# Opening of an attention block: silu moved to VectorE, one tile normalized by ScalarE, the third query copied by VectorE, the warm-up matmuls and first loads rearranged, and TensorE's usual path placed behind its branch without a jump

## The chip, the cores and the metric

One core of one Trainium2 chip. The metric is the device time of one execution in microseconds (us); lower is better. An execution also has a span, the stretch that the profile covers; the time is about 1.7 to 1.9 us more than the span.

## The reference, cut to what matters

```python
mod = (_silu(c) @ w_mod).reshape(c.shape[0], 6, 1, -1)      # c: 1 x 512, w_mod: 512 x 3072
sa, ca, ga, sb, cb, gb = ...                                # six rows of 512
h = _layernorm(x) * (1 + ca) + sa                           # x: 2048 x 512
x = x + ga * _A_ref(h, k_cache, v_cache, wq, wo)            # 32 query heads, 8 key heads of 128,
                                                            # softmax over the last 512 keys
h = _layernorm(x) * (1 + cb) + sb
x = x + gb * _B_ref(h, w1, w2)                              # relu MLP of width 1792
```

The first score matmul needs three things: x normalized, transposed, scaled and shifted; the scale and shift (`sa`, `ca`), which need silu(c) and a megabyte of `w_mod`; and the first query weights. That opening is what the change is about. At the other end, the softmax is computed without subtracting a maximum; a flag says whether that was safe, and each engine branches on it before its last instructions (TensorE at 510.6 us of the 559.4 in the profile below).

## The kernel before

TensorE is PE, VectorE DVE, ScalarE ACT, GpSimd POOL, SyncE SP; SP and ACT issue the loads. The program keeps one list of instructions for each engine; `reads` and `writes` become semaphores.

```python
def load_wm01(i, eng=None):                  # half of the shift and scale weights, 512 KB
    c0, c1 = i * DC // 2, (i + 1) * DC // 2
    dma(wm01[:, c0:c1, :], wm01v[:, c0:c1, :], f"wm{i}", writes=[R_wm[i]], eng=eng)

def warm(n):                                 # the warm-up: matmuls on ones
    for i in range(n):
        mm(bank[WBK], ones[:, :], ones[:, 0:1].to_broadcast([P, QB]), True, True, [R_ones], [WBK], i == n - 1)

def silu_mul():                              # c / (1 + exp(-c)); the power -1 by cst[:, 3:4]
    kb.op(POOL, ... tensor_scalar(tmp, tmp, 1e38, 1.0, op0=min, op1=add))
    kb.op(POOL, ... tensor_tensor(tmp, tmp, cst[:, 3:4], op=pow))
    kb.op(POOL, ... tensor_tensor(sc_bf, c_f, tmp, op=mult))
# ... cut ...
    load_wm01(0); load_wm01(1, ACT); load_wq(0, 2, ACT); load_wq(2, 2); load_k(0); load_v(0)
    warm(7)
    silu_exp(5)                              # transpose of c on PE; exp and copy on ACT
    warm(9)
    # ... ACT: sum and sum of squares of tile 3 ...
    silu_mul()
    ln_stat(0); ln_stat(1)                   # DVE
    rstd_add(0, 2); rstd_pow(0, 2)           # DVE, then POOL: (var + eps) ** -0.5
    ln_stat(2)
    rstd_add(2, 3); rstd_pow(2, 4)
    ln_norm(0); ln_norm(1)                   # DVE; tile 3 is normalized by POOL
    ln_tposes(0, TB[0])                      # transposes on PE
    for f in mod_cols_mm(0, QBK): f()        # 32 one-column matmuls: shift and scale
    ln_norm(2)
    mod_cols_evac(0, QBK)
    # ... transposes of tiles 1 to 3, scaling (hT), first two queries (qT) ...
# ... cut ...
def engine(name, e):
    kb.emit(stream, e, 0, n_ops)
    # ... wait for the flag ...
    v = e.value_load(flag[0:1, 0:1])
    with e.If(v != 128):                     # never in these runs
        kb.emit(stream, e, n_ops)
        # ... all engines meet ...
        gkb.emit(general[name], e)           # the general kernel, long
    with e.Else():
        kb.emit(stream, e, n_ops)            # the last part
```

Of the kernel before, what the change touches and what calls it, by code (L numbers as in the profile page):

```python
# [8 lines left out]
ACTF = mybir.ActivationFunctionType  # L9
# [1189 lines left out]
def build_fast(nc, es, top, A_x, A_k_cache, A_v_cache, A_wq, A_wo, B_x, B_w1, B_w2, c, w_mod, out, flag):  # L1199
    P = 128  # L1200
# [98 lines left out]
    def dma(out_ap, in_ap, key, reads=(), writes=(), transpose=False, eng=None):  # L1299
        k = dsem(key)  # L1300
        if transpose:
            return kb.op(SP, lambda e: e.dma_start_transpose(out_ap, in_ap), reads=reads, writes=writes, dma_sem=k)
        return kb.op(eng or SP, lambda e: e.dma_start(out_ap, in_ap), reads=reads, writes=writes, dma_sem=k)  # L1303
# [14 lines left out]
    R_h0 = RL("h0", DC)  # L1318
    R_q1 = RL("q1_", 2)
    R_cf, R_m01 = Res("cf"), Res("m01")  # L1320
    R_s3, R_eps = Res("s3"), Res("eps")
# [28 lines left out]
    def load_wm01(i, eng=None):  # L1350
        c0, c1 = i * DC // 2, (i + 1) * DC // 2
        dma(wm01[:, c0:c1, :], wm01v[:, c0:c1, :], f"wm{i}", writes=[R_wm[i]], eng=eng)

    def wm_res(sl, cc):
        return R_wm[cc // (DC // 2)] if sl < 2 else R_wm[sl]

# [5 lines left out]
    def load_mlp(i):  # L1362
        if not wm_done:
            wm_done.extend(all_events(R_wm))
        f0 = i % (FC // 2) * 2
        if i < FC // 2:
            kb.op(SP, lambda e: e.dma_start(w1_sb[:, :, f0 * P:(f0 + 2) * P], w1v[:, :, f0 * P:(f0 + 2) * P]), writes=R_w1[f0:f0 + 2], pre=wm_done, dma_sem=dsem(f"w1{f0}"))
        else:
            kb.op(SP, lambda e: e.dma_start(w2_sb[:, f0:f0 + 2, :], w2v[:, f0:f0 + 2, :]), writes=R_w2[f0:f0 + 2], pre=wm_done, dma_sem=dsem(f"w2{f0}"))
# [6 lines left out]

    def warm(n):
        for i in range(n):
            mm(bank[WBK], ones[:, :], ones[:, 0:1].to_broadcast([P, QB]), True, True, [R_ones], [WBK], i == n - 1)

# [39 lines left out]
    def silu_mul():  # L1420
        kb.op(POOL, lambda e: e.tensor_scalar(tmp[:, :], tmp[:, :], 1e38, 1.0, op0=ALU.min, op1=ALU.add), reads=[R_tmp], writes=[R_tmp])
        kb.op(POOL, lambda e: e.tensor_tensor(tmp[:, :], tmp[:, :], cst[:, 3:4].to_broadcast([P, DC]), op=ALU.pow), reads=[R_tmp, R_eps], writes=[R_tmp])
        kb.op(POOL, lambda e: e.tensor_tensor(sc_bf[:, :], c_f[:, :], tmp[:, :], op=ALU.mult), reads=[R_tmp, R_cf], writes=[R_sc])

# [52 lines left out]
    def q_mms(u, bk=QBK):  # L1477
        b, h = units[u]
        for i, cc in enumerate(range(DC)):
            mm(bank[bk], wq_sb[:, cc, h * Dh:(h + 1) * Dh], hT[b % 2][:, cc, :], i == 0, i == DC - 1,  # L1480
               [R_wq[h], R_hT[b % 2][cc]] + ([R_h0[cc]] if b == 0 else []), [bk], i == DC - 1)
        q_evac(u, bk)

    def q_evac(u, bk=QBK):
        kb.op(ACT, lambda e: e.activation(qT[u % NQT][:, :], bank[bk], ACTF.Copy), reads=[R_b[bk]], writes=[R_qT[u % NQT]])  # L1485

# [74 lines left out]
    dma(c_row[:, :], c[0].rearrange("(c p) -> c p", p=P), "c", writes=[R_c])  # L1561
    load_wm01(0)
    load_wm01(1, ACT)
    load_wq(0, 2, ACT)
    load_wq(2, 2)
    load_k(0)
    load_v(0)
    kb.op(POOL, lambda e: e.memset(ones[:, :], 1.0), writes=[R_ones])
    kb.op(POOL, lambda e: e.memset(cst[:, 0:1], -0.5), writes=[R_cst])
# [7 lines left out]
    kb.op(ACT, lambda e: e.activation(cst[:, 2:3], cst[:, 0:1], ACTF.Exp), reads=[R_cst], writes=[Res("dummy")])  # L1577
    warm(7)
    silu_exp(5)
    warm(9)  # L1580
    t3 = TPB - 1
    kb.op(ACT, lambda e: e.activation(xn[:, t3, :], x_sb[:, t3, :], ACTF.Copy, accum_out=s3[:, 0:1]), reads=[R_x[t3]], writes=[R_xn[t3], R_s3])
    kb.op(ACT, lambda e: e.activation(s3[:, 1:2], s3[:, 0:1], ACTF.Copy, scale=-1.0 / D), reads=[R_s3], writes=[R_s3])
    kb.op(ACT, lambda e: e.activation(xn[:, t3, :], x_sb[:, t3, :], ACTF.Square, bias=s3[:, 1:2], accum_out=s3[:, 2:3]), reads=[R_x[t3], R_s3], writes=[R_xn[t3], R_s3])
    kb.op(ACT, lambda e: e.activation(rstd[:, t3:t3 + 1], s3[:, 2:3], ACTF.Identity, scale=1.0 / D, bias=cst[:, 1:2]), reads=[R_s3, R_eps], writes=[R_rstd[t3]])
# [7 lines left out]

    silu_mul()
    ln_stat(0)
    ln_stat(1)
    rstd_add(0, 2)
    rstd_pow(0, 2)
    ln_stat(2)
    rstd_add(2, 3)  # L1600
    rstd_pow(2, 4)
    ln_norm(0)
    ln_norm(1)
    kb.op(POOL, lambda e: e.tensor_scalar(xn[:, t3, :], x_sb[:, t3, :], s3[:, 1:2], rstd[:, t3:t3 + 1], op0=ALU.add, op1=ALU.mult),
# [9 lines left out]

    ln_tposes(0, TB[0])
    fs = mod_cols_mm(0, QBK)
    for f in fs:
        f()
    ln_norm(2)
    mod_cols_evac(0, QBK)  # L1620
# [13 lines left out]
    def q_half(u, hf, order, bk):  # L1634
        for cc in order:
            mm(bank[bk][:, hf * HB:(hf + 1) * HB], wq_sb[:, cc, u * Dh:(u + 1) * Dh], hT[0][:, cc, hf * HB:(hf + 1) * HB], cc == CC_ORDER[0], cc == CC_ORDER[-1],
               [R_wq[u], R_half[hf][cc]], [bk], cc == CC_ORDER[-1])

    for tl in range(1, TPB):
        ln_tposes(tl, TB[tl // 2])  # L1640
    mod_half(0, 0, DVE)
    mod_half(0, 2, ACT)
    mod_half(0, 1, DVE)
    mod_half(0, 3, ACT)
# [61 lines left out]
    def h1_group(b, fc):  # L1706
        dst, r = h2_of[b]
        bk = hb_banks[cnt["h"] % len(hb_banks)]
        cnt["h"] += 1
        for cc in range(DC):  # L1710
            mm(bank[bk], w1_sb[:, cc, fc * P:(fc + 1) * P], dst[:, cc, :], cc == 0, cc == DC - 1, [R_w1[fc], r[cc]], [bk], cc == DC - 1)
        kb.op(ACT, lambda e: e.activation(h1T[b % 2][:, fc, :], bank[bk], ACTF.Relu), reads=[R_b[bk]], writes=[R_h1[b % 2][fc]],  # L1712
              pre=all_events(R_wq) if b < 2 else ())

# [86 lines left out]
def bass_adaLN_cond__sliding_block_cached__dense_activation_relu__prompt_kernel(  # L1801
# [14 lines left out]
    with ExitStack() as top:  # L1816
# [5 lines left out]
        with ExitStack() as es:  # L1822
            gkb, general = build_general(nc, es, *args)

            def engine(name, e):
                stream, n_ops = fast[name], cut[name]
                kb.emit(stream, e, 0, n_ops)
                e.wait_ge(sems[flag_ev[0]], flag_ev[1])
                v = e.value_load(flag[0:1, 0:1])
                with e.If(v != 128):  # L1830
                    kb.emit(stream, e, n_ops)
                    if stream.cnt:
                        e.wait_ge(sems[name], stream.cnt)
                    if name == "sp":
                        for k, n in dma_cnt.items():
                            e.wait_ge(sems[k], n)
                    e.sem_inc(meet, 1)
                    e.wait_ge(meet, len(fast))
                    gkb.emit(general[name], e)
                with e.Else():  # L1840
                    kb.emit(stream, e, n_ops)

# [50 lines left out]
```

## Time and profile before

| | before |
|---|---|
| time, median of 3 (lowest to highest) | 560.52 us (560.33 to 560.81) |
| the profiled execution: time, span | 561.1, 559.4 us |
| first value product's weights loaded at | 16.47 us |
| last VectorE instruction to the end of the span | 2.02 us |

The first value product is the first matmul of softmax times V. From there to the branch TensorE is dense, so this moment measures the opening. The lines of the page and of the chain are in the prediction.

### The profile page before, as it was taken

What the parts mean: (1) busy time and instruction counts of PE and PEld (TensorE: products, weight loads), DVE (VectorE), ACT (ScalarE), POOL (GpSimd) and SP (SyncE); (2) the same over time, 40 slices, a digit from 0 to 9 for tenths busy, and PEclk for the clock granted to TensorE, in tenths of its full rate; (3) what the DMA queues carried; (4) which work ended last, traced back from release to release, by engine and by line L of the source; (5) the groups of instructions that cost most, each with busy time, mean ns of one, the idle gap of its engine ahead of it and who ended that gap; (6) DMA issues with size and microseconds to landing.
All of it is one profiled execution on the core that took longest, in us unless ns stands there. A gap on an engine that the chain in (4) does not pass through costs nothing.

```text
span 559.4 us, 9666 instructions
## 1 busy us (share of the span) xinstructions
PE 550.5 (98%) x4060; PEld 315.8 (56%) x4134; DVE 253.8 (45%) x551; ACT 348.9 (62%) x453; POOL 54.7 (10%) x53
## 2 busy tenths in 40 slices
PE   8999999999999999999999999999999999999998
PEld 4665555555555555555555555555555654444444
DVE  4455555553546544335445443333354448321134
ACT  4986666666666666666666666666666644432500
POOL 3000022004410000033000000332000000000000
DMA  9897763513114144352352412111215110210001
GB/s 268 248 207 174 143 169 46 114 39 76 40 38 76 39 73 117 58 133 57 94 95 57 76 40 39 39 39 38 39 39 76 39 30 0 44 34 23 22 29 47
DMA packets 113309, 42.67 MB, mean 76 GB/s; under 512 B 93928, under 2 KB 112104, under 8 KB 113256
## 3 DMA queue, kind: packets, MB, share of 16 engines
q1 hardware_dynamic: 112024, 40.82, 34.3%
q10 hardware_dynamic: 1232, 1.15, 0.6%
q8 instruction: 33, 0.54, 0.4%
q14 instruction: 20, 0.16, 0.1%
HBM read 18.35 MB, written 2.10 MB: 37 GB/s over the span
## 4 chain that ended last, share of the span: by engine, by line
PE 98%; issue 1%; DMA 1%; DVE 0%; SPq 0%; DVEq 0%
PE psS L1372 28%; PE psO L1372 27%; PE psQ L1372 23%; PE psW L1372 20%; DMA c_row<-in_c_dram 1%; DVE qT L1611 0%; DVE hT L1630 0%; SPq L1303 0%; DVE PT L1723 0%; DVE PT L1725 0%; PE psS L1375 0%; PE psO L1416 0%; DVE modc L1438 0%; DVEq L123 0%
## 5 line engine op out<-in xcount | busy, mean ns | idle before, releaser
L1493 ACT ACTIVATE PT<-psS 128x1024 bf16<-128x1024 f32 x256 | 262.7, 1028 | 128.2 <-PE psS L1372 128.1
L1372 PE MATMUL psS<-qT,kT 128*128 128x512 bf16 x508 | 150.9, 379 | 0.5 <-DVE qT L1611 0.4
L1372 PEld LDWEIGHTS psO<-v,PT 128*128 128x128 bf16 x2048 | 126.6, 98 | 30.2
L1372 PE MATMUL psO<-v,PT 128*128 128x129 bf16 x2048 | 137.0, 220 | 0.0
L1372 PE MATMUL psQ<-hT,wq 128*128 128x512 bf16 (+1 forms) x510 | 130.5, 377 | 0.3 <-DVE hT L1630 0.2
L1503 DVE RECIPROCAL rinv<-psO 128x4 f32<-128x4 f32 x128 | 23.3, 182 | 227.2 <-PE psO L1372 227.2
L1372 PE MATMUL psW<-wo,oT 128*128 128x512 bf16 x454 | 118.1, 379 | 3.0
L1504 DVE TENSOR_TENSOR o<-psO,rinv 128x512 bf16<-128x512 f32 x128 | 88.5, 691 | 4.9 <-DVE rinv L1503 0.5
L1372 PEld LDWEIGHTS psQ<-hT,wq 128*128 128x128 bf16 x512 | 49.9, 98 | 60.3 <-issue 0.6
L1372 PEld LDWEIGHTS psS<-qT,kT 128*128 128x128 bf16 x512 | 49.5, 98 | 58.9 <-ACT PT L1493 0.7
L1485 ACT ACTIVATE qT<-psQ 128x512 bf16<-128x512 f32 x126 | 74.7, 593 | 0.0
L1712 ACT ACTIVATE wq<-psS 128x512 bf16<-128x512 f32 x56 | 33.4, 597 | 49.3 <-PE psS L1372 48.9
L1372 PEld LDWEIGHTS psW<-wo,oT 128*128 128x128 bf16 x512 | 45.0, 98 | 32.9 <-DVE acc L1526 1.2
L1526 DVE TENSOR_TENSOR acc<-psW,acc 128x512 f32<-128x512 f32 x48 | 33.2, 691 | 6.5 <-PE psW L1372 6.5
L1372 PE MATMUL psO<-wmw,wq 128*128 128x512 bf16 (+1 forms) x165 | 32.8, 352 | 0.3
L1529 POOL TENSOR_TENSOR acc<-acc,gaf 128x512 f32<-128x512 f32 x12 | 15.6, 1303 | 146.7 <-DVE acc L1526 139.8
L1388 POOL TENSOR_TENSOR rstd<-rstd,cst 128x4 f32<-128x4 f32 x7 | 7.2, 1025 | 216.8 <-DVE rstd L1387 216.8
L1723 DVE TENSOR_TENSOR PT<-psO,gbf 128x512 f32<-128x512 f32 (+1 forms) x12 | 7.5, 624 | 40.4 <-PE psO L1372 40.4
L1372 PE MATMUL psS<-h2T,wmw 128*128 128x512 bf16 x109 | 25.0, 379 | 0.2
L1372 PEld LDWEIGHTS psO<-wmw,wq 128*128 128x128 bf16 x168 | 15.3, 98 | 16.5
L1372 PE MATMUL psS<-hT,wmw 128*128 128x512 bf16 x110 | 24.4, 379 | 0.1
L1382 DVE BATCH_NORM_STATS2 st<-x 128x6 f32<-128x512 bf16 x31 | 21.1, 681 | 4.8 <-DMA x<-in_A_x_dram 4.8
(85 smaller groups left out, 192.6 us busy)
## 6 DMA issues: line engine op xcount, KB each, us to landing
wo<-in_A_wo_dram SPq DMA_DIRECT2D x4, 1024.0 KB, 5.9
wq<-in_A_wq_dram SPq DMA_DIRECT2D x7, 512.0 KB, 4.6
wmw<-in_B_w_dram SPq DMA_DIRECT2D x14, 256.0 KB, 3.1
wmw<-in_w_mod_dram SPq DMA_DIRECT2D x5, 512.0 KB, 4.8
oT<-o SPq DMA_TRANSPOSE x128, 2.4
out_dram<-PT SPq DMA_DIRECT2D x15, 128.0 KB, 1.7
x<-in_A_x_dram SPq DMA_DIRECT2D x3, 512.0 KB, 4.3
v<-in_A_v_cache_dram SPq DMA_DIRECT2D x8, 128.0 KB, 3.8
```

Source lines behind the costliest of these rows:

```text
L1372: kb.op(PE, lambda e: e.matmul(out_ap, lhsT, rhs, start=start, stop=stop), reads=reads, group_writes=[R_b[k] for k in bk], signal=signal)
L1382: kb.op(DVE, lambda e: e.bn_stats(st[:, t, :], x_sb[:, t, :]), reads=[R_x[t]], writes=[R_st[t]])
L1388: kb.op(POOL, lambda e: e.tensor_tensor(rstd[:, sl], rstd[:, sl], cst[:, 0:1].to_broadcast([P, hi - lo]), op=ALU.pow), reads=R_rstd[sl] + ...
L1485: kb.op(ACT, lambda e: e.activation(qT[u % NQT][:, :], bank[bk], ACTF.Copy), reads=[R_b[bk]], writes=[R_qT[u % NQT]])
L1493: kb.op(ACT, lambda e: e.activation(PT[u % NPT][:, pr * 2:pr * 2 + 2, :], s_ps[pr][:, :, :], ACTF.Exp, scale=scale), reads=[R_b[pr * 2], R ...
L1503: kb.op(DVE, lambda e: e.reciprocal(rinv[:, u, :], o_ps[:, :, P]), reads=[R_b[5], R_b[6]], writes=[R_rinv])
L1504: kb.op(DVE, lambda e: e.tensor_tensor(o_sb[u % NOS][:, :, :], o_ps[:, :, 0:P], rinv[:, u, :].unsqueeze(2).to_broadcast([P, TPB, P]), op=A ...
L1526: kb.op(DVE, lambda e: e.tensor_tensor(acc[:, tl, :], bank[WBK], acc[:, tl, :], op=ALU.add), reads=[R_b[WBK], R_acc[tl]], writes=[R_acc[tl]])
L1529: kb.op(eng, lambda e: e.tensor_tensor(acc[:, tl, :], acc[:, tl, :], gaf[:, :], op=ALU.mult), reads=[R_acc[tl], R_ga], writes=[R_acc[tl]])
L1712: kb.op(ACT, lambda e: e.activation(h1T[b % 2][:, fc, :], bank[bk], ACTF.Relu), reads=[R_b[bk]], writes=[R_h1[b % 2][fc]], pre=all_events( ...
L1723: kb.op(DVE, lambda e: e.tensor_tensor(yt[i][:, c0:c1], bank[bk][:, c0:c1], gbf[:, c0:c1], op=ALU.mult), reads=[R_b[bk], R_gb], writes=[R_ ...
```

## The change

Its intent is to take the silu off GpSimd (whose power for it took 1.04 us), to stop warm-up matmuls from holding TensorE (until 8.98) when silu(c) is ready (at 7.12), to spread normalization over three engines, and to spare TensorE a jump (its branch took 3.44 us). The diff, cut to its core:

```diff
     def load_wm01(i, eng=None):
-        c0, c1 = i * DC // 2, (i + 1) * DC // 2
-        dma(wm01[:, c0:c1, :], wm01v[:, c0:c1, :], f"wm{i}", writes=[R_wm[i]], eng=eng)
+        dma(wm01[:, i, :], wm01v[:, i, :], f"wmc{i}", writes=[R_wmc[i]], eng=eng)
...
-    def warm(n):
+    def warm(n, gate=(), bk=7):            # gate: also wait for these
...
     def silu_mul():                        # POOL add, pow, mult -> DVE add, reciprocal, mult
...
     def q_evac(u, bk=QBK):
+        if u == QA:                        # the third query
+            kb.op(DVE, lambda e: e.tensor_copy(qT[u % NQT][:, :], bank[bk]), ...)
+            return
...
-    load_wm01(0)
-    load_wm01(1, ACT)
-    load_wq(0, 2, ACT)
+    for i in range(DC):
+        load_wm01(i, (ACT, SP)[i % 2])
+    for i, eng in enumerate((SP, SP)):     # first query weights in two pieces
+        dma(wq_sb[:, 2 * i:2 * i + 2, 0:QA * Dh], ..., eng=eng)
+    load_k(0)
     load_wq(2, 2)
-    load_k(0)
...
-    kb.op(POOL, ... memset(ones, 1.0))
+    kb.op(DVE, ... memset(ones, 1.0))
...
-    warm(7)
-    silu_exp(5)
-    warm(9)
     # ACT: sum of tile 3
+    warm(10)
+    silu_exp(5)
...
-    silu_mul()
     ln_stat(0)
+    warm(3, [R_mv[0]])
     ln_stat(1)
+    warm(2, [R_mv[1]])
     rstd_add(0, 2)
     rstd_pow(0, 2)
+    kb.op(POOL, ... s3[:, 3:4] = -mean(1) * rstd(1))
+    kb.op(ACT, lambda e: e.activation(xn[:, 1, :], x_sb[:, 1, :], ACTF.Identity, bias=s3[:, 3:4], scale=rstd[:, 1:2]), ...)
+    silu_mul()
     ln_stat(2)
...
-    ln_norm(1)
...
-    ln_tposes(0, TB[0])
     # the 32 matmuls of the modulation
-    ln_norm(2)
+    ln_tposes(0, TB[0])
...
+    ln_tposes(1, TB[0])
+    warm(2, bk=6)
+    ln_norm(2)
...
+                if name == "pe":
+                    with e.If(v == 128):
+                        last_part()
+                    with e.Else():
+                        rerun()
+                else:                      # as before
```

More of the change, by code (lines that the diff above doesn't have):

```diff
@@ L1319, in build_fast @@
     R_q1 = RL("q1_", 2)
+    R_wmc = RL("wmc", DC)
+    R_wqa = RL("wqa", 2)
+    R_nmr = Res("nmr")
     R_cf, R_m01 = Res("cf"), Res("m01")
@@ L1350, in load_wm01 @@
     def load_wm01(i, eng=None):
-        c0, c1 = i * DC // 2, (i + 1) * DC // 2
-        dma(wm01[:, c0:c1, :], wm01v[:, c0:c1, :], f"wm{i}", writes=[R_wm[i]], eng=eng)
+        dma(wm01[:, i, :], wm01v[:, i, :], f"wmc{i}", writes=[R_wmc[i]], eng=eng)
     def wm_res(sl, cc):
-        return R_wm[cc // (DC // 2)] if sl < 2 else R_wm[sl]
+        return R_wmc[cc] if sl < 2 else R_wm[sl]
     def load_wo(j):
@@ L1363, in load_mlp @@
         if not wm_done:
-            wm_done.extend(all_events(R_wm))
+            wm_done.extend(all_events(R_wm + R_wmc))
         f0 = i % (FC // 2) * 2
@@ L1375, in tpose @@
         kb.op(PE, lambda e: e.transpose(out_ap, in_ap, ident[:, :]), reads=list(reads) + [R_ident], group_writes=[R_b[k] for k in bk], signal=signal)
-    def warm(n):
+    def warm(n, gate=(), bk=7):
         for i in range(n):
-            mm(bank[WBK], ones[:, :], ones[:, 0:1].to_broadcast([P, QB]), True, True, [R_ones], [WBK], i == n - 1)
+            mm(bank[bk], ones[:, :], ones[:, 0:1].to_broadcast([P, QB]), True, True, [R_ones] + list(gate), [bk], i == n - 1)
     def ln_stat(t):
@@ L1420, in silu_mul @@
     def silu_mul():
-        kb.op(POOL, lambda e: e.tensor_scalar(tmp[:, :], tmp[:, :], 1e38, 1.0, op0=ALU.min, op1=ALU.add), reads=[R_tmp], writes=[R_tmp])
-        kb.op(POOL, lambda e: e.tensor_tensor(tmp[:, :], tmp[:, :], cst[:, 3:4].to_broadcast([P, DC]), op=ALU.pow), reads=[R_tmp, R_eps], writes=[R_tmp])
-        kb.op(POOL, lambda e: e.tensor_tensor(sc_bf[:, :], c_f[:, :], tmp[:, :], op=ALU.mult), reads=[R_tmp, R_cf], writes=[R_sc])
+        kb.op(DVE, lambda e: e.tensor_scalar(tmp[:, :], tmp[:, :], 1e38, 1.0, op0=ALU.min, op1=ALU.add), reads=[R_tmp], writes=[R_tmp])
+        kb.op(DVE, lambda e: e.reciprocal(tmp[:, :], tmp[:, :]), reads=[R_tmp], writes=[R_tmp])
+        kb.op(DVE, lambda e: e.tensor_tensor(sc_bf[:, :], c_f[:, :], tmp[:, :], op=ALU.mult), reads=[R_tmp, R_cf], writes=[R_sc])
     def mod_cols_mm(which, bk):
@@ L1480, in q_mms @@
             mm(bank[bk], wq_sb[:, cc, h * Dh:(h + 1) * Dh], hT[b % 2][:, cc, :], i == 0, i == DC - 1,
-               [R_wq[h], R_hT[b % 2][cc]] + ([R_h0[cc]] if b == 0 else []), [bk], i == DC - 1)
+               (R_wqa if h < QA else [R_wq[h]]) + [R_hT[b % 2][cc]] + ([R_h0[cc]] if b == 0 else []), [bk], i == DC - 1)
         q_evac(u, bk)
     def q_evac(u, bk=QBK):
+        if u == QA:
+            kb.op(DVE, lambda e: e.tensor_copy(qT[u % NQT][:, :], bank[bk]), reads=[R_b[bk]], writes=[R_qT[u % NQT]])
+            return
         kb.op(ACT, lambda e: e.activation(qT[u % NQT][:, :], bank[bk], ACTF.Copy), reads=[R_b[bk]], writes=[R_qT[u % NQT]])
@@ L1561, in build_fast @@
     dma(c_row[:, :], c[0].rearrange("(c p) -> c p", p=P), "c", writes=[R_c])
-    load_wm01(0)
-    load_wm01(1, ACT)
-    load_wq(0, 2, ACT)
+    for i in range(DC):
+        load_wm01(i, (ACT, SP)[i % 2])
+    for i, eng in enumerate((SP, SP)):
+        dma(wq_sb[:, 2 * i:2 * i + 2, 0:QA * Dh], wqv[:, 2 * i:2 * i + 2, 0:QA * Dh], f"wqa{i}", writes=[R_wqa[i]], eng=eng)
+    load_k(0)
     load_wq(2, 2)
-    load_k(0)
     load_v(0)
-    kb.op(POOL, lambda e: e.memset(ones[:, :], 1.0), writes=[R_ones])
+    kb.op(DVE, lambda e: e.memset(ones[:, :], 1.0), writes=[R_ones])
     kb.op(POOL, lambda e: e.memset(cst[:, 0:1], -0.5), writes=[R_cst])
@@ L1592, in rstd_pow @@
               reads=R_rstd[lo:hi] + [R_cst], writes=R_rstd[lo:hi])
-    silu_mul()
     ln_stat(0)
+    warm(3, [R_mv[0]])
     ln_stat(1)
+    warm(2, [R_mv[1]])
     rstd_add(0, 2)
     rstd_pow(0, 2)
+    kb.op(POOL, lambda e: e.tensor_scalar(s3[:, 3:4], mv[:, 1, 0:1], rstd[:, 1:2], -1.0, op0=ALU.mult, op1=ALU.mult), reads=[R_mv[1], R_rstd[1]], writes=[R_nmr])
+    kb.op(ACT, lambda e: e.activation(xn[:, 1, :], x_sb[:, 1, :], ACTF.Identity, bias=s3[:, 3:4], scale=rstd[:, 1:2]),
+          reads=[R_x[1], R_nmr, R_rstd[1]], writes=[R_xn[1]])
+    silu_mul()
     ln_stat(2)
@@ L1636, in q_half @@
             mm(bank[bk][:, hf * HB:(hf + 1) * HB], wq_sb[:, cc, u * Dh:(u + 1) * Dh], hT[0][:, cc, hf * HB:(hf + 1) * HB], cc == CC_ORDER[0], cc == CC_ORDER[-1],
-               [R_wq[u], R_half[hf][cc]], [bk], cc == CC_ORDER[-1])
-    for tl in range(1, TPB):
-        ln_tposes(tl, TB[tl // 2])
+               [R_wqa[cc // 2], R_half[hf][cc]], [bk], cc == CC_ORDER[-1])
+    ln_tposes(1, TB[0])
+    warm(2, bk=6)
+    ln_norm(2)
     mod_half(0, 0, DVE)
     mod_half(0, 2, ACT)
+    ln_tposes(2, TB[1])
+    ln_tposes(3, TB[1])
     mod_half(0, 1, DVE)
@@ L1712, in h1_group @@
         kb.op(ACT, lambda e: e.activation(h1T[b % 2][:, fc, :], bank[bk], ACTF.Relu), reads=[R_b[bk]], writes=[R_h1[b % 2][fc]],
-              pre=all_events(R_wq) if b < 2 else ())
+              pre=all_events(R_wq + R_wqa) if b < 2 else ())
     def y_group(b, tl, c0=0, c1=D, deng=None):
@@ L1829, in engine, with last_part, rerun @@
                 v = e.value_load(flag[0:1, 0:1])
-                with e.If(v != 128):
+                def last_part():
+                    kb.emit(stream, e, n_ops)
+                def rerun():
                     kb.emit(stream, e, n_ops)
@@ L1839, in engine @@
                     gkb.emit(general[name], e)
-                with e.Else():
-                    kb.emit(stream, e, n_ops)
+                if name == "pe":
[4 more added lines that the diff above has]
+                else:
+                    with e.If(v != 128):
+                        rerun()
+                    with e.Else():
+                        last_part()
             with nc.allow_non_contiguous_dma(reason="tiny c vector load in column layout, value rows of 256 bytes"):
```

## The prediction

> **What bounds the kernel now.** I first read the page's table of busy time. It puts TensorE (PE) at 98%, and its 40 slices show a 9 everywhere but at the two ends.
>
> ```profile
> PE 550.5 (98%) x4060; PEld 315.8 (56%) x4134; DVE 253.8 (45%) x551; ACT 348.9 (62%) x453; POOL 54.7 (10%) x53
> PE   8999999999999999999999999999999999999998
> ```
>
> So only the part before TensorE becomes dense, or a gap in its stream, can change the time. Busy is not useful, though: warm-up matmuls on a tile of ones count as busy. The chain of waits, in order of time, names what sets the opening:
>
> ```profile
> 1.24 3.66 DMA c_row<-in_c_dram
> 4.90 0.05 issue
> 4.95 0.18 PE psO L1416
> 5.13 3.86 PE psW L1372 x9
> 8.98 0.22 PE psS L1375 x4
> 9.21 0.79 PE psQ L1372 x32
> 10.00 0.02 issue
> 10.02 0.18 DVE modc L1438
> ...
> 10.30 0.42 DVE hT L1630
> ...
> 12.55 0.44 DVE qT L1611
> 12.99 0.35 issue
> 13.34 0.38 PE psS L1372
> ```
>
> The columns are start, duration and what. The row of c lands at 4.90; nine warm-up matmuls then hold TensorE until 8.98, although silu(c), needed by the 32 matmuls of the modulation, is ready at 7.12 (POOL's last silu multiply runs 6.92 to 7.12 in the timeline). Modulation, scaling of the transposed tiles (hT), the first projection (psQ) and its copies (qT) follow one another until the first score matmul at 13.34. From there the chain is matmul after matmul: value products of successive units start at 16.84, 19.48, 22.11, 24.75, a step of 2.635 us, which is what 8 matmuls of 0.216 and 16 of 0.057 cost. The stretch 13.34 to 16.84 is 3.50 us for 16 such matmuls, 3.45 us of work: only 0.05 us lost. The tail is equally dense. Hence the time moves by as much as the first score matmul moves, plus a few hundredths.
>
> The timeline of that opening gives the other lanes:
>
> ```profile
> 4.79 0.69 DVE L1382 BATCH_NORM_STATS2 st<-x 128x6 f32<-128x512 bf16 x1 [4.79 <-DMA x<-in_A_x_dram]
> 5.80 1.04 POOL L1422 TENSOR_TENSOR tmp<-tmp,cst 128x4 f32<-128x4 f32 x1
> 7.08 1.51 POOL L1591 TENSOR_TENSOR rstd<-rstd,cst 128x2 f32<-128x2 f32 x2
> 8.70 0.90 POOL L1604 TENSOR_SCALAR xn<-x,s,rstd 128x512 bf16<-128x512 bf16 x1
> ```
>
> GpSimd (POOL) does the silu power in 1.04 us, then two powers for the layer norm (0.75 each), then normalizes tile 3 until 9.60. That lane is free of waits from 5.43 on, so GpSimd is nearly as late as the warm-up.
>
> [...] warm-up weight loads follow at 0.43 us (5.46, 5.89, 6.32 ... 8.02), while later 128x512 matmuls take 0.216 us. The four transposes at 8.98 take 0.22 us, so the full clock came between 8.45 and 8.98. [...] the power takes 1.04 us on GpSimd, against 182 ns for VectorE's 128x4 reciprocal. [...] the trace has 721 ns for the square with a bias. [...] ACT, POOL, SP and DVE take 50 to 72 ns but PE 3440 ns, from 510.6. That ends at 514.05, just before the queued matmuls run out at 514.12; the chain shows 0.03 us of issue there.
>
> **The change, part by part.**
>
> *Warm-up.* It was 7 + 9 matmuls with c's transpose between, and becomes 10, transpose, then 3 and 2 that wait for the statistics of tiles 0 and 1, plus 2 more between transposes. VectorE now fills the ones, so the start stays near 1.0. Cold, ten take 4.27 us, to 5.3; c's transpose is then at 5.3, but ScalarE's exponential is now behind the tile-3 sum and its scaling (about 5.0 to 5.95) anyway. The last five end at 7.0 if the clock is up by then, at 7.9 if not. They no longer hold the modulation until 8.98.
>
> *Silu.* Removed from GpSimd: 0.28 + 1.04 + 0.20 us. Added to VectorE: add, reciprocal, multiply, each 0.17 to 0.18 us and stepping by 0.22. VectorE's statistics of tiles 0 and 1 and the eps add end at 6.70 as before; silu ends near 7.21, within 0.1 us of the old 7.12. So silu itself gains nothing, but tile 2's statistics slip from 6.60 to 7.11, and the add behind them ends at 8.20 instead of 7.69.
>
> *Modulation.* The shift and scale weights arrive in four 256 KB pieces. In the trace the half issued by SP at 1.66 landed 6.3 us later, at 7.96; now ScalarE's queue no longer carries the first query weights beside it, so I take 7.2 to 7.9 for the last piece. The 32 matmuls (0.79 us) end by 8.2, against 10.00.
>
> *GpSimd lane.* First power at 6.75, done 7.50; the small product for ScalarE's bias (0.28, as silu's first step) done near 7.89; second power waits for VectorE's 8.20: 8.25 to 9.00; tile 3 from 9.10 (the old gap was 0.11) to 10.00. It ended at 9.60 before: **0.40 us later**.
>
> *Normalized tiles.* Tile 0 on VectorE 8.12 to 8.53; [...] tile 2 on VectorE behind the second power, 9.04 to 9.45. Transposes of tiles 0, 1, two warm-ups, tile 2 fill TensorE to about 9.7; tile 3's then run 10.05 to 10.27. Before, the last transpose ended at 10.68 in the profile's modelled ends; with the same 0.17 us of drain, now 10.44. VectorE's two first-half scalings run from 9.47, with modulation long ready (8.75), so they no longer sit in front of the second-half ones.
>
> *From there.* Second-half scalings on VectorE, steps of 0.32 and a last of 0.40: 10.47, 10.79, 11.11 to 11.51. Before, the last ended at 11.99: **-0.48 us**. From that end to the first score matmul the old chain needs 13.34 - 11.99 = 1.35 us and is unchanged, so the first score matmul is at 12.86.
>
> *Third query by VectorE.* It takes 0.59 us off ScalarE in the first unit, where the old trace lost 0.05 us. **-0.05 us**. VectorE was idle there until 17.79.
>
> *Branch in place.* TensorE falls through to its usual path. The visible gap was 0.03 us: **-0.03 us**, in an unprofiled run perhaps a little more.
>
> Sum: -0.48 - 0.05 - 0.03 = -0.56 us, that is 560.52 - 0.56 = 559.96. I shade it to 559.9, because a slightly earlier start and a little more at the branch are likelier than a longer lane.
>
> **The rivals.** *The modulation is the end of the chain, and all its lead counts.* The modulation matmuls end 1.8 us earlier, and one would then expect 558.7. Against it: tile 3 on GpSimd goes 0.40 us later, and everything behind needs all four tiles. I believe the lead is turned into this new wait. *The clock stays half.* The warm-up is cut into 10 + 5 and later work is sparse: from 7.2 to 10.3 TensorE has only 1-column matmuls, transposes and two warm-ups. If it falls back or never reaches full clock, the 16 first projection matmuls of 256 columns cost 0.21 instead of 0.11 us, 1.7 us together, and the time becomes 561 to 562. For it: in the old trace the first 3 us of warm-up were not enough. Against: ten matmuls are 4.3 us without a break. *A transfer gates.* The key tile and third query weights are issued about 0.8 and 3 us later; if the weights still take the old 7.1 us they land at 12.3, and they are needed about 13.2. Little margin, about 0.5 us if it fails. *The far branch at the end:* TensorE now jumps over the general code after its last matmul. If that costs the 3.4 us seen at the other branch, it runs from 555.5 to about 559.0, just hidden behind SP's last steps at 559.1.
>
> **Range and chances.** Lanes differ by 0.3 us each way in such chains, and the three old runs by 0.48 us. Most results between 559.2 and 560.7. The half-clock rival makes the upper tail, the modulation rival the lower. A 2% change is 11.2 us, nearly the whole opening: faster 0.003, same 0.992, slower 0.005.
>
> **What would show each step.** Right if modulation ends near 8.2 with TensorE then waiting for normalized tiles, tile 3 ends on GpSimd at 10.0, the last scaling ends near 11.5, the first score matmul stands at 12.9, the value products again step by 2.635, and no gap shows at TensorE's branch. Wrong if 256-column projections step by 0.21 us (clock), if a score or third-query matmul waits for a transfer, if GpSimd's powers are much shorter or longer than 0.75 us, or if the span changes after the first score matmul by more than 0.2 us.

The forecast's sum came to -0.56 us, that is 559.96 us shaded to 559.9. The 0.43 and 0.216 us are the evidence for a clock at half at first. That ten warm-up matmuls without a break are enough to bring it up was my estimate; the trace did not show it. The 50 to 72 ns and the 3440 ns are those of the compare-and-branch instructions. Tile 1: its time on ScalarE is in no term of the sum (the trace of the changed kernel has 0.81 us for it, 7.74 to 8.55).

## The result, and the profile after

The changed kernel takes 560.66 us (median of 5, 560.32 to 560.73), the kernel before 560.68 us (5 runs beside it, 560.33 to 561.45). The ratio is 0.9997, with a 95% interval of 0.9982 to 1.0012: the same. Ratios here are the mean time of one kernel's fast runs over that of the other's of the same rounds, so not quite the ratio of the medians quoted. The number lies inside the predicted range, but the 0.56 us that the working found do not show. All outputs are right.

The page of the changed kernel, its busy time and TensorE's slices:

```profile
PE 549.5 (98%) x4061; PEld 315.5 (56%) x4135; DVE 254.7 (46%) x555; ACT 349.3 (63%) x453; POOL 53.3 (10%) x50
PE   8999999999999999999999999999999999999997
```

Nothing changes between the ends; the last slice has lost a tenth. The chain of waits of its opening (start, duration, what):

```profile
6.85 0.16 DVE sc_bf L1425
7.01 0.62 DVE st L1384
...
7.87 0.17 DVE rstd L1593
8.11 0.81 POOL rstd L1596
9.02 0.91 POOL xn L1613
9.97 0.34 PE psS L1377 x3
10.37 0.44 PE psQ L1374 x4
10.81 1.00 PE psO L1374 x8
11.84 0.44 DVE qT L1620
12.27 0.14 issue
12.41 0.59 PE psS L1374 x2
```

As predicted, the chain no longer passes through the warm-up or the modulation. Silu is ready at 7.01; tile 2's statistics (`st`) come behind it, then GpSimd's second power and tile 3 (`xn`, ending at 9.93), then TensorE and the copies. The first score matmul is at 12.41 instead of 13.34.

Part of that is no gain. The group of score matmuls has 508 records before and 510 after, and the program issues 512:

```profile
L1372 PE MATMUL psS<-qT,kT 128*128 128x512 bf16 x508 | 150.9, 379 | 0.5 <-DVE qT L1611 0.4
```
```profile
L1374 PE MATMUL psS<-qT,kT 128*128 128x512 bf16 x510 | 151.4, 379 | 0.3 <-DVE qT L1620 0.2
```

One of the missing ones is the first: the old chain's "12.99 0.35 issue" ahead of "13.34 0.38 PE psS" is a lost record, where the new one has 0.14 and two matmuls in 0.59. The old first score matmul was really at about 12.99 + 0.14 = 13.13 (an estimate from that same 0.14). Weight loads give the honest figure: the first value product's weights were loaded at 16.47 before and 15.74 after.

At the other end the branch lines (which engine's sequencer, count, shortest, mean and longest ns, from when to when) and the output transfers of the last 5 us (KB each, us from issue to landing), first of the kernel before:

```profile
L1830 PEldq COMPARE_BRANCH  x1: 3440/3440/3440, 510.6 to 510.6; - x1
...
out_dram<-PT ACTq DMA_DIRECT2D x1, 64.0 KB, 1.6
out_dram<-PT SPq DMA_DIRECT2D x1, 32.0 KB, 1.5
out_dram<-PT ACTq DMA_DIRECT2D x1, 32.0 KB, 1.5
```

and of the changed kernel:

```profile
L1857 PEldq COMPARE_BRANCH  x2: 90/1850/3610, 509.9 to 554.6; - x2
...
q8 instruction: 2, 0.03, 2.7%
out_dram<-PT ACTq DMA_DIRECT2D x1, 64.0 KB, 2.7
out_dram<-PT SPq DMA_DIRECT2D x1, 32.0 KB, 2.4
out_dram<-PT ACTq DMA_DIRECT2D x1, 32.0 KB, 1.9
```

TensorE falls through in 90 ns at 509.9, but at 554.6 it has to jump over the general code, 3.61 us. The jump itself ends at 558.2, before the span does. But with it come two packets of 16 KB on the instruction queue (`q8`), which the kernel before has about its branch in the middle and not here; the first of them (555.61 to 556.86) falls among the output transfers, the second starts when they have landed. The three last outputs take 1.9 to 2.7 us to land instead of 1.5 to 1.6. The last of them is what ends the program.

So for this pair of executions: opening 15.74 - 16.47 = -0.73, branch (the 40 matmuls about it take 8.63 instead of 8.84 us) -0.21, ending (from VectorE's last instruction to the end, 2.44 instead of 2.02) +0.42. The sum is -0.52, the spans say 558.86 - 559.36 = -0.50. A saving of 0.5 us in the profiles, and none in the timed runs: either the two executions are not typical, or something escapes the profile.

### The profile page after: what moved, and what is told of

The parts are those of the page before. It is cut to its first block, busy times and chain, and to the rows that moved or that the text cites. A ratio compares the mean times of both kernels' runs of the same rounds, so it can differ in the third digit from the quotient of the medians.

```text
span 558.9 us, 9675 instructions
## 1 busy us (share of the span) xinstructions
PE 549.5 (98%) x4061; PEld 315.5 (56%) x4135; DVE 254.7 (46%) x555; ACT 349.3 (63%) x453; POOL 53.3 (10%) x50
## 4 chain that ended last, share of the span: by engine, by line
PE 97%; issue 1%; DVE 1%; DMA 1%; POOL 0%
PE psS L1374 28%; PE psO L1374 27%; PE psQ L1374 23%; PE psW L1374 19%; DMA x<-in_A_x_dram 1%; DVE st L1384 0%; POOL xn L1613 0%; POOL rstd L1596 0%; DVE mv L1385 0%; DVE qT L1620 0%; PE psS L1377 0%; DVE rstd L1593 0%; DVE PT L1734 0%; DVE PT L1736 0%; DVE tmp L1424 0%
## 5 line engine op out<-in xcount | busy, mean ns | idle before, releaser
L1534 POOL TENSOR_TENSOR acc<-acc,gaf 128x512 f32<-128x512 f32 x12 | 15.6, 1301 | 146.8 <-DVE acc L1531 139.8
```

Of the source, the lines that this page charges most:

```text
L1534: kb.op(eng, lambda e: e.tensor_tensor(acc[:, tl, :], acc[:, tl, :], gaf[:, :], op=ALU.mult), reads=[R_acc[tl], R_ga], writes=[R_acc[tl]])
```

## The experiments

**Theory.** One execution of either kernel is not the kernel: the moment at which the clock comes up, and transfers, move the opening by as much as the change is worth, and the profiled execution of the kernel before was a slow one. What is steady is small: a little won at the branch and rather more lost at the end. **Rivals:** the split loads make the shift and scale weights land later; one of the parts costs what another wins (silu, tile 1 or the third query); the clock falls back to half.

All profiles fit one sum: span = first value product's weight load + the 40 matmuls about the branch + ending + 532.05 us, within 0.02 us in each of the 14. The rest of the kernel is the same in all of them. The table gives the three terms of each kernel's profiled execution.

| kernel | loads | TensorE's branch | weight load of first value product | branch stretch | ending | span |
|---|---|---|---|---|---|---|
| before | old | old | 16.47 | 8.84 | 2.02 | 559.36 |
| b_again | old | old | 15.64 | 8.84 | 2.02 | 558.55 |
| b_newbranch | old | new | 16.67 | 8.63 | 2.26 | 559.61 |
| b_warm10_6 | old | old | 17.25 | 8.82 | 2.02 | 560.12 |
| after | new | new | 15.74 | 8.63 | 2.44 | 558.86 |
| a_again | new | new | 16.16 | 8.63 | 2.42 | 559.26 |
| a_again2 | new | new | 15.83 | 8.63 | 2.19 | 558.70 |
| a_oldbranch | new | old | 16.33 | 8.90 | 2.00 | 559.27 |
| a_oldloads | old | new | 15.88 | 8.63 | 2.45 | 559.01 |
| a_oldloads_oldbranch | old | old | 16.27 | 9.20 | 2.02 | 559.53 |
| a_q3act | new | new | 15.92 | 8.63 | 2.61 | 559.20 |
| a_silupool | new | new | 17.91 | 8.63 | 2.42 | 561.00 |
| a_xn1dve | new | new | 15.65 | 8.63 | 2.30 | 558.63 |
| a_best | old | old | 15.72 | 8.77 | 2.01 | 558.55 |

Names with b are the kernel before with an edit, those with a the changed kernel. Twelve kernels ran, in three groups, each group on one chip.

### The kernels as they are, again: b_again, a_again, a_again2

No edit.

> The kernel before, unchanged, to learn how far one profile of it stands for others. Theory (its first profile, 559.4 us, was a slow instance): its time is again about 560.6 us, but the spans of its executions spread over 0.5 us or more (from about 558.7 to 559.5), and the gap at TensorE's branch or the moment of full clock differs from the first profile (0.21 us at the branch, full clock by 8.5 to 9.0). Rival (the profile is typical): spans within 0.2 us of 559.4, the same 0.21 us at the branch, first value product (weight load) at 16.47, and then the time of the changed kernel should be 0.5 us lower, which it was not.

Measured: 560.31 us, ratio to the kernel before 1.0001 (0.9988 to 1.0014). That the time is the same was bound to be; the profile is the point. The chain of its opening:

```profile
4.83 3.14 PE psW L1372 x9
...
12.30 0.59 PE psS L1372 x2
```

The same nine warm-up matmuls took 3.86 us in the first profile and held TensorE until 8.98; here they take 3.14, because the clock came up at about 7.0 (their weight loads step by 0.43 us up to 6.87, and the last three take 0.60 together), and end at 7.97 (they also start 0.30 us earlier, as the row of c was there earlier). The first score matmul is at 12.30 and the span 0.81 us shorter, with not a line changed. That is more than the whole change was predicted to bring.

> The changed kernel, unchanged. Theory: ratio 0.999 to 1.000, first value product's weight load at 15.74 within 0.1, no gap at the branch, and 2.4 us from VectorE's last instruction to the end of the span. Rival (the long ending was chance): 2.0 us there, as in the kernel before, and the span 0.4 us shorter than 558.9.

Measured: 560.75 us, ratio 1.0005 (0.9992 to 1.0018). The profile of this execution has another chain than the first one of the changed kernel:

```profile
2.05 7.00 DMA wmw<-in_w_mod_dram
9.09 0.35 PE psQ L1374 x8
...
12.83 0.59 PE psS L1374 x2
```

The last piece of the shift and scale weights landed at 9.05 instead of 7.92, and the modulation became the end of the chain: first score matmul at 12.83. In that profile the rate of all transfers falls from about 300 GB/s at 7 us to about 20 from 8.7 to 9.6, a sixteenth of the 350 reached at other times: as much as one of the core's 16 DMA engines moves (an estimate).

> The changed kernel once more, as the comparison for the next three on the same chip. Theory (two endings of the opening: GpSimd's tile 3 when the modulation weights land by 8, their landing when it comes after 9): either last piece at 7.9 to 8.0 and the first value product's weight load at 15.7 to 15.95, or at 9.0 to 9.2 and 16.1 to 16.4. Rival: anything between, or a late opening with weights landed early.

Measured: 560.70 us on another chip, ratio 1.0002 (0.9988 to 1.0017), last piece at 7.63, earlier than either branch of the theory had it, weight load at 15.83, inside the first.

What follows: with the executions timed beside all the experiments there are 31 of the kernel before at full clock, with spans from 558.3 to 559.5 and a mean of 558.74; the first profile, at 559.4, is slower than all but one of them. The changed kernel has 15, from 558.5 to 559.3, mean 558.85. The difference is +0.11 us, with a standard error of 0.07 (standard deviations 0.26 and 0.20); on the two chips that ran both it is +0.25 and +0.10.

### The branch alone: a_oldbranch, b_newbranch

```diff
# a_oldbranch: the changed kernel with
-                if name == "pe":
-                    with e.If(v == 128):
-                        last_part()
-                    with e.Else():
-                        rerun()
-                else: ...
+                with e.If(v != 128):
+                    rerun()
+                with e.Else():
+                    last_part()
# b_newbranch: the kernel before with the same edit the other way round
```

> The changed kernel with TensorE's usual path again behind the general code, as before; nothing else undone. Theory (the jump over the general code at the end fetches instructions while the last outputs are on the DMA engines): the 0.2 us gap at the branch is back, the stretch from VectorE's last instruction to the end of the span is back to 2.0 us from 2.4, so the span is 0.2 us shorter than the changed kernel's and the time about 0.2 us lower. Rival (the ending varies by chance, and the branch in place is a gain): 0.2 us slower than the changed kernel, ending as the changed kernel's.

Measured: 560.84 us, ratio 1.0010 (0.9998 to 1.0022). The branch stretch is 8.90 and the ending 2.00 us, and the three outputs land after 1.6, 1.5 and 1.5 us, as in the kernel before. The time is not lower all the same: in the profiled execution the last piece of the modulation weights landed at 9.21 and cost the opening some 0.6 us against the first profile, and one of its six executions ran at a mean granted clock of 0.997.

> The kernel before with the branch in place and nothing else. Theory: opening as before (weight load of the first value product at 16.47), no gap at the branch (-0.2 us), the ending longer by 0.4 us; time 0.2 us above the kernel before. Rival (branch in place gains): 0.03 to 0.2 us faster, ending 2.0 us.

Measured: 560.51 us, ratio 1.0000 (0.9987 to 1.0013). The branch stretch is 8.63, 0.21 less than in the kernel before; the ending 2.26, 0.24 more; the outputs land after 2.5, 2.2 and 1.7 us, the first of two instruction packets beside them. The time, expected 0.2 us higher, is the same.

What follows: each end of the branch's effect is shown from both sides. Over all profiles, six with the old branch have a mean stretch of 8.90 and a mean ending of 2.01; eight with the new one 8.63 and 2.38. The new branch wins 0.27 us in the middle and loses 0.37 at the end. The two together are 0.1 us worse with a standard error of about 0.08: no gain, and a loss that is likely rather than shown. The timed ratios, uncertain by some 0.7 us each way, cannot tell.

The packets of the traces show where the outputs wait. Each of the three is 144 packets. In all eight profiles with the new branch 135 packets of the first output start on time, and the other nine, a sixteenth, only when the first instruction packet ends (556.84 and 556.86 us in the changed kernel, within 0.02 us in all eight); nine of the second output follow behind them. The third, on the queue of the first, starts after those in the changed kernel, 1.28 us after its issue instead of 0.86. In the six with the old branch none is late, and no instruction packet is there. So the nine seem to wait behind the instruction packet, on one of the 16 DMA engines (an estimate from their share, 9 of 144). The second instruction packet, at 558.99, starts after the last output has landed (558.36) and does nothing.

### The loads: a_oldloads, a_oldloads_oldbranch

```diff
-    for i in range(DC):
-        load_wm01(i, (ACT, SP)[i % 2])          # pieces of 256 KB
-    for i, eng in enumerate((SP, SP)):
-        dma(wq_sb[:, 2 * i:2 * i + 2, 0:QA * Dh], ..., eng=eng)
-    load_k(0)
+    load_wm01(0)                                # halves of 512 KB
+    load_wm01(1, ACT)
+    load_wq(0, 2, ACT)
     load_wq(2, 2)
+    load_k(0)
# a_oldloads_oldbranch: also the branch as in a_oldbranch
```

> The changed kernel with the old loads of modulation and first query weights (two halves of 512 KB, first query weights on ScalarE's queue); the rest of the change, branch included, kept. Theory (the new loads made a new wait: in three profiles of the changed loads the last modulation piece landed at 7.92, 9.05 and 9.21, against 7.8 to 8.0 for the old loads in three profiles): the last half lands at 7.8 to 8.0 again, the modulation matmuls end by 8.3, GpSimd's tile 3 sets the opening, first value product's weight load at 15.7 within 0.15; time 0.1 to 0.4 us below the changed kernel's. Rival (the late landing belongs to the chip or the day, not to the order of loads): landing at 9 or later in this one too, weight load at 16.2.

Measured: 560.71 us, ratio 1.0001 (0.9985 to 1.0016), so the expected gain in time does not show. The last half landed at 7.87, but the 32 modulation matmuls ran from 8.00 to 8.94 and did not end by 8.3; the weight load was at 15.88, and GpSimd's tile 3 (ready at 10.06) set the opening, as in the first profile of the changed kernel.

> The same with TensorE's usual path behind the general code as before. Theory: weight load of the first value product at 15.7, 0.2 us lost at the branch, 2.0 us from VectorE's last instruction to the end; time 0.2 us below the run with old loads alone, and 0.2 to 0.4 us below the kernel before. Rival: landing as in the rival above, and then no better than the kernel before.

Measured: 560.66 us, ratio 0.9994 (0.9980 to 1.0008). Its profiled execution opens late (16.27, not 15.7): the last half landed only at 8.21, the modulation ended at 9.29, and VectorE's second normalization, behind it, took 0.82 us and ended after tile 3. Its branch stretch, 9.20, is the longest of all.

What follows: with the old loads the last piece landed between 7.76 and 8.23 in seven profiles; with the new ones it landed between 7.63 and 8.34 in five and at 9.05 and 9.21 in two, both on the same chip, on which the old loads landed at 7.79 and 8.02. Late landing was seen with the new loads alone, but two in seven on one chip do not prove that the split is the cause, and the timed ratios do not separate the two. It stays open.

### The warm-up: b_warm10_6

```diff
# the kernel before with
-    warm(7)
+    warm(10)
     silu_exp(5)
-    warm(9)
+    warm(6)
```

> The kernel before with its 16 warm-up matmuls split 10 + 6 instead of 7 + 9; nothing else. Theory (in the kernel before the full clock comes at 7.0 in one profile and only after 8.5 in two, which moves the first value product from 15.64 to 16.47 and 16.67; ten matmuls without a break bring it by 4.6, as in all three profiles of the changed opening): six later warm-ups step by 0.22, modulation waits for its weights or silu, not for warm-ups, and the first value product's weight load is at 15.6 or earlier in this profile; executions spread less, time at or 0.2 us below the kernel before. Rival (the clock's coming is chance): late clock again, 16.5, no gain.

Measured: 561.36 us, ratio 1.0007 (0.9992 to 1.0023); the kernel before had 560.84 there. The first half of the expectation holds: after ten matmuls without a break the clock is up by 4.3, and the six that follow step by 0.22. The second half does not, for this reason. The stretches of this kernel's profile (from:to, length, then busy us and instructions of PE, PEld, DVE, ACT, POOL, then granted clock, DMA share, GB/s):

```profile
10.00:11.00 1.00, 0.90 (x8) 0.43 (x6) 1.00 (x4) 1.00 (x3) 0.00 (x0) 0.91 1.11 296
11.00:12.00 1.00, 1.00 (x6) 0.75 (x5) 0.44 (x2) 0.60 (x2) 0.00 (x0) 0.50 1.15 321
```

From 10.83 the granted clock is 0.50, until 14.24. The warm-up had ended early and TensorE was busy for 0.34 us between 6 and 8. Two of its five executions ran at a mean clock of 0.997, with spans of 560.1 and 560.5; the two at 1.0 had 558.9 and 559.2. This is the rival of the prediction, "the clock stays half", in the form that it falls back. That the split makes it more frequent is not shown: of the nine executions of the kernel before beside it, three had 0.997 too. (A mean of 0.997 is 3.4 us at half clock in a span of 559, an estimate.)

When the clock comes up can be read from the clock records of the traces (13 of the 14 have them; the first profile of the kernel before has none). Here the clock changes at 4.00, 10.83 and 14.24 us, in a_silupool below at 7.01, 10.42 and 13.83: the changes are one or two steps of 3.41 us apart. With the changed opening, warm from 1.10 us on, it rose at 3.90 to 4.71 in six profiles and at 6.30 to 7.01 in four. In b_newbranch, where TensorE waited for the row of c until 4.80, the rise came only at 10.00. So ten matmuls without a break do not bring the clock by 4.6 in every execution, as I had expected. What decides between an early and a late rise is not shown.

The fall does not follow from idle time alone: by the busy times of the 1 us stretches TensorE stood idle for 1.26 us from 7 to 10 here and for 0.77 in a_silupool, and the clock fell in both; in the profile of a_best it stood idle for 0.85 there, and the clock stayed full. In a_silupool the busy share of these stretches was 0.82, 0.91 and 0.50. What decides it stays open.

### One part at a time: a_q3act, a_xn1dve, a_silupool

```diff
# a_q3act: the third query copied by ACT, as before
-        if u == QA:
-            kb.op(DVE, lambda e: e.tensor_copy(qT[u % NQT][:, :], bank[bk]), ...)
-            return
```

> The changed kernel with the third query copied by ScalarE again. Theory (nothing is gained there: from the first score matmul to the first value product both kernels take 3.7 us once the score matmul missing from the first trace of the kernel before is allowed for): time within 0.1 us of the changed kernel, 3.7 us for that stretch. Rival (my prediction): 3.75 to 3.8 us, 0.05 us slower.

Measured: 560.75 us, ratio 0.9997 (0.9984 to 1.0011). From the first score matmul to the first value product it takes 3.55 us, the changed kernel 3.55, b_again (old copy) 3.55; the 3.7 of the expectation was measured to a later mark. The part is worth nothing.

```diff
# a_xn1dve: tile 1 normalized by DVE, as before
-    kb.op(POOL, ... s3[:, 3:4] = -mean(1) * rstd(1))
-    kb.op(ACT, ... xn[:, 1, :] ...)
...
     ln_norm(0)
+    ln_norm(1)
```

> The changed kernel with tile 1 normalized by VectorE again and the small GpSimd product for ScalarE's bias left out; nothing else undone. Theory (tile 1 is off the path: GpSimd's second power waits for VectorE's add at about 8.0, not for the small product): tile 3 ready at the same 9.9 to 10.1, opening within 0.1 us. Rival (ScalarE's share is what pays): opening 0.3 to 0.4 us later, one 128x512 normalization on VectorE.

Measured: 560.53 us, ratio 0.9998 (0.9983 to 1.0014), weight load at 15.65 and span 558.63; the mean span of its four executions, 558.8, is that of the changed kernel on this chip. ScalarE's tile wins nothing; the 0.81 us that it takes run beside the others, but VectorE's slot that it frees was not on the chain, and GpSimd has to compute the product for it.

```diff
# a_silupool: the silu on POOL, ahead of the statistics, as before
-        kb.op(DVE, ... add) ; kb.op(DVE, ... reciprocal) ; kb.op(DVE, ... mult)
+        kb.op(POOL, ... add) ; kb.op(POOL, ... pow) ; kb.op(POOL, ... mult)
...
+    silu_mul()
     ln_stat(0)
...
-    silu_mul()
     ln_stat(2)
```

> The changed kernel with silu on GpSimd again, as GpSimd's first work; nothing else undone. Theory (silu only changes which lane feeds GpSimd's tile 3: with it on GpSimd the lane is 1.5 us of silu, 0.75, 0.26, 0.8, 0.9; with it on VectorE tile 2's statistics wait): silu ready at 7.2 to 7.3, tile 3 ready at 10.1 to 10.3 instead of 9.9 to 10.1, opening 0.1 to 0.3 us later than the changed kernel's when the weights land early. Rival (silu on VectorE is what makes the opening shorter): opening 0.5 us later or more.

Measured: 562.61 us, ratio 1.0029 (1.0013 to 1.0045): slower by 2.1 us than the kernel before's 560.52, and the one clear difference. Stretches and chain of its profile:

```profile
10.00:11.00 1.00, 1.00 (x12) 0.76 (x10) 0.73 (x2) 0.84 (x2) 0.50 (x1) 0.71 1.25 259
11.00:12.00 1.00, 1.00 (x8) 0.80 (x7) 0.55 (x2) 0.73 (x2) 0.00 (x0) 0.50 1.09 344
```
```profile
11.41 0.85 PE psQ L1374 x4
12.26 1.72 PE psO L1374 x8
```

Tile 3 is ready on GpSimd at 10.50, about 0.5 us later, which is the loss that the lane explains. The rest is the clock: it is at half from 10.42 to 13.83, and the same projections that took 0.44 and 1.00 us in the changed kernel take 0.85 and 1.72. All four executions had a mean clock of 0.996 or 0.997, against two of eleven of the kernel before beside them. Why this order of work brings the fall is not shown. My expectation counted the lane alone and missed the larger term.

### A version meant to beat both: a_best

```diff
# the changed kernel with old loads and old branch, and
-    silu_mul()
     ln_stat(2)
     rstd_add(2, 3)
+    silu_mul()                      # DVE, behind tile 2's statistics
...
     ln_tposes(1, TB[0])
-    warm(2, bk=6)
```

> A version put together from what the runs showed: the changed kernel with the old loads, the old branch, silu on VectorE after tile 2's statistics, and without the two warm-ups between the transposes. Theory: last modulation half at 7.8 to 8.2, tile 3 ready by 9.6, first value product's weight load at 15.4 to 15.6, ending 2.0 us: 0.2 to 0.4 us below the kernel before. Rival (with fewer warm-ups TensorE falls back to half clock, as in the run with 10 + 6): a granted clock of 0.5 between 10 and 14 in the profile or 0.997 for some executions, and a time 0.5 to 1 us above.

Measured: 561.22 us, ratio 1.0013 (0.9995 to 1.0031). Three of its six executions are at full clock, with spans of 558.4, 558.5 and 558.7, below the means of both kernels; the other three, at 0.997, have 560.2, 560.4 and 561.1. Tile 3 is ready at 9.31 as intended, but the modulation (ending at 9.05) and VectorE's normalizations then set the opening, and the weight load comes at 15.72, not 15.4 to 15.6. The lead is a few tenths at most, and the clock fell back in half of the executions; in the changed kernel in one of 16, in the kernel before in five of 36 (two of the eleven on this chip). The two missing warm-up matmuls are a possible reason, but three of six against two of eleven may also be chance; the modulation is later here too, and no run separates these. No version beats both.

## Why the prediction was right or wrong

It held where it counted: the same time, within the range (560.66 in 559.2 to 560.7), and the bound was the right one. That it lies inside has luck in it: it is 0.04 us from the upper end, which was put there for a half clock, and the central 559.9 rests on a gain that is not there. Point by point:

**The opening's lane: right.** Predicted and measured in the first profile of the changed kernel: silu 7.21 and 7.01; modulation matmuls ending 8.2 and about 8.3; second power ending 9.00 and 8.91; tile 3 at 10.00 and 9.92; last scaling 11.51 and 11.46. That the lead of the modulation would turn into a wait for tile 3 on GpSimd was right.

**The reference point: wrong, and the step that failed most.** The "-0.48 us" was taken as a difference from one execution of the kernel before, in which the warm-up lasted until 8.98. That execution was one of the slowest; b_again's opening is 0.83 us earlier without an edit. The steady terms explain it: the mean spans of 558.74 and 558.85, less 532.05 and the mean branch stretch and ending of each kernel's kind, leave 558.74 - 532.05 - 8.90 - 2.01 = 15.78 and 558.85 - 532.05 - 8.63 - 2.38 = 15.79 us for the typical weight load (estimates, each good to about 0.1). The opening gains nothing that can be measured. What the change did remove is the warm-up from the chain: when the clock comes late, as in the first profile and in b_newbranch (16.67), the old kernel waits for it. In the ten profiles with the changed opening the step of the warm-up matmuls falls from 0.43 to 0.22 us between 3.6 and 4.8 in six, and only between 6.1 and 7.2 in four; of those four, a_again2, a_oldloads and a_best have their weight load at 15.83, 15.88 and 15.72 all the same.

**From the last scaling to the first score matmul, "1.35 us and unchanged": wrong.** It is 0.95. About 0.21 was the missing record; the other 0.19 is the copy starting 0.38 us behind the last scaling instead of 0.56.

**Third query, "-0.05 us": wrong**, it is nothing; the 3.50 us that it came from were measured from a start that had lost its first record (13.34 for about 13.13) to the chain's mark of 16.84, where the first value product's own record stands at 16.68: 3.55 us, as in every other profile at full clock.

**Branch, "-0.03 us": wrong in size, and likely in sign.** I counted the gap that the chain of waits shows, which follows a modelled end (513.74 + 0.38). From start to start the two matmuls at the branch are 0.41 us apart (513.74 and 514.15) instead of 0.22; over six profiles the loss is 0.14 to 0.57 us, 0.27 in the mean. And the rival at the end, put as "just hidden", was half right: the jump is hidden, its effect on the last outputs' landing is not, and the ending grows by 0.37. The two together are +0.1 us, with a standard error of about 0.08.

Two readings of the trace were slightly off and changed nothing: the old half of the modulation weights landed at 7.91, not 7.96, and PE's branch ended at 514.09, not 514.05.

**The rivals.** The modulation as the end of the chain came true in a_again and a_oldbranch, because of a late transfer, not because the rest was fast. A gating transfer was expected at the key tile or the third query weights and came at the modulation weights instead; its cause is open. The fall to half clock did not hit the changed kernel as a rule (one execution in 16), but it lay close: the kernel before met it in five of 36, five of the experiments in at least one execution, a_silupool in all four.

So the predicted 0.56 us went three ways: most was never there, being the bad luck of the one profile of before; 0.05 was a missing record; and the branch, counted as a gain, is none, and likely a loss of about 0.1 us.

## What to carry to other kernels

A change worth half a microsecond can't be read as the difference of two profiles when an unchanged kernel moves by 0.8: take the profile of before twice, and look at whether the chain passes through something that varies, such as a clock coming up (here at 3.9 to 10.0 us) or a transfer (landing at 7.6 to 9.2). A branch has two ends: placing the usual path without a jump at the head moved the jump to the tail here, where its 3.61 us met the last outputs and the ending grew by 0.37 us in the mean. Where TensorE's work is sparse, count the executions at a lower mean clock as well as the profile's waits before taking warm-up matmuls out, and count them for the unchanged kernel on the same chip too (here three of six of a_best at 0.997, and two of eleven of the kernel before).
